# Row scatters, two pieces of expert work and a drain of Pool: one change to a fused attention and mixture-of-experts kernel

## The chip, the cores and the metric

The kernel runs on one core of a Trainium2 chip (trn2). The metric is device time in microseconds, from the first instruction to the last. Every run here was compared with the reference and was correct. A run counts as fast when it lies within 1.5% of the fastest run of the same kernel, else as slow. The ratio of two kernels is the mean time of one kernel's fast runs over that of the other's of the same rounds, so it isn't quite the ratio of the medians quoted beside it. A ratio below 1 means that the new kernel is faster; the brackets hold a 95% interval.

One thing that the text needs early, although it was only learnt from the runs: the chips that served this case came in two kinds. The kernel before takes 196 us on one kind and 235 us on the other. The words "fast chip" and "slow chip" below mean these two kinds and have nothing to do with fast and slow runs. No chip was seen as both kinds, and one (number 8) was slow in two batches 46 minutes apart; whether the cause lies in the chip or in what surrounds it, no run shows.

## The reference, cut to what matters

Block attention whose keys and values are first mixed between blocks by a Sinkhorn-normalised matrix; its output rows go through a top-1 mixture of eight experts.

```python
# attention: B, H, S, D = 4, 8, 768, 64; eight blocks of 96 positions
scores = scale * np.matmul(q_b, k_sb.transpose(0, 1, 2, 4, 3))
attn = softmax(scores)                      # the reference writes it out
x = (attn @ v_sb) -> [3072, 512]            # rows: batch and position; columns: heads
# experts: N, D, E, F = 3072, 512, 8, 1024
logits = x @ w_gate + modality_bias[modality_id]
e_idx = np.argmax(logits, axis=1)
for e in range(E):
    mask = e_idx == e
    h = np.maximum(x[mask] @ w1[e], 0.0)
    out[mask] = gate_w[mask, None] * (h @ w2[e])
```

## The kernel before

The attention is done in 32 units, eight to a group; a group is a quarter of the rows. When a group's eight units are done, its gate is computed in four parts (`gate_T` transposes a quarter of the columns, `gate_L` makes the logits), `choose` picks each row's expert, and `place(m)` computes a destination for each row and scatters the rows, with eight indirect DMAs of Pool, to a scratch array in DRAM that is sorted by expert. Slots of 256 rows of one expert are then loaded back and multiplied: `mL1` is the first expert layer, `mL2` the second, and each `mL2` ends in an indirect DMA of Pool that writes 128 rows of the result.

These pieces of expert work are spread between the attention units to fill TensorE's gaps:

```python
    def run_pieces(n):
        for _ in range(n):
            ...                               # (cut) stop if the slot's rows have not been asked for
            f(*a)
            if f is mL1 and a[1] == 3:
                st["l1"] = a[0] + 1
            if f is mL2 and a[1] == 1:
                st["done"] = a[0] + 1
            x_try()
            st["pos"] += 1

    def pace(u):
        return (0, 0) if u < 16 else (1, 0)

    for u in range(2, 32):
        p1, p2 = pace(u)
        scores(u)
        expo(u)
        run_pieces(p1)
        for f, a in A1.get(u, []):            # gate_L, place, ...
            f(*a)
        av(u - 1)                             # product op, norm xb = op * rs
        prep_q(u + 2)
        prep_s(u + 3)
        run_pieces(p2)
        for f, a in A2.get(u, []):            # gate_T: transposes gt of xb
            f(*a)
    run_pieces(1)
    av(31)
    gate_L(3, 2)
    run_pieces(2)
    gate_T(3, 3)
    run_pieces(1)
    gate_L(3, 3)
    choose(3)
    run_pieces(2)
    place(3)
    run_pieces(2)
    table_x(3)
    run_pieces(8)
    # (cut) a branch that is rarely taken, then the rest of the pieces
```

And the scatters of one group, with padding between them that is meant to have "rows leave at an even pace":

```python
        def one(t):
            if t:
                if m:
                    for _ in range(11):
                        nc.gpsimd.nop(nofuse=True)
                nc.gpsimd.nop()
            ins = nc.gpsimd.indirect_dma_start(
                out=xs_dram, out_offset=bass.IndirectOffsetOnAxis(ap=dest[:, t:t + 1], axis=0),
                in_=xt.bitcast(I32)[:, t], in_offset=None)
        for t in range(8):
            one(t)
```

The softmax here doesn't subtract the row's maximum and nothing guards it: scores larger than these inputs give would overflow.

## Time and profile before

| | us |
|---|---|
| median of three runs | 234.14 (233.84 to 235.94) |
| span of the profiled run | 191.1 |
| TensorE's last product in that run | ends at 181.6 |
| end of that product to end of program | 9.5 |

The page of the profiled run gives busy tenths in 40 equal slices of the span (some 4.8 us each), and below them the clock that the throttle granted TensorE:

```profile
span 191.1 us, 5316 instructions
PE   6594597888499989899799999987999999999900
POOL 7921296970075103576057741776044223232320
PEclk9969969999859999999999999999999999999975
```

The reader is to see that TensorE is busy for 7 tenths or more of every slice from the 12th (some 53 us) on, at nine tenths of the clock or more from the 13th, until two slices of nothing at the end. The 43 us between the span and the median were unexplained when the prediction was made. By all later runs they are two chips: the profile came from a fast one, the three timed runs from a slow one (the record gives no chip numbers for these first runs, so this is read from their times). The record of the profile already said something: its own execution was timed at 192.78 us, only 1.7 above its span.

### The profile page before, as it was taken

The page shows a single profiled execution, that of the slowest core. Times are in us where ns is not written, and L with a number is a line of the kernel's source. Part 1 is how long each engine was busy: PE and PEld are TensorE (multiplying, and loading weights), DVE is VectorE, ACT ScalarE, POOL GpSimd, SP SyncE. Part 2 cuts the span into 40 slices and gives each one's busy share as a digit, 9 for nine tenths or more (in the row PEclk, how much of TensorE's full clock was granted, in tenths as well). Part 3 has the DMA queues.
Part 4 walks back from the last instruction along what each step waited for, and adds up shares of the span by engine and source line. Part 5 has one row for each costly group of instructions (what it writes and reads, how often), then busy time and mean ns, then how long its engine had stood idle before and what let it go on. Part 6 is the DMA issues. An engine that isn't in the chain of part 4 may idle for free.

```text
span 191.1 us, 5316 instructions
## 1 busy us (share of the span) xinstructions
PE 160.8 (84%) x2127; PEld 122.1 (64%) x2127; DVE 100.6 (53%) x332; ACT 93.4 (49%) x149; POOL 83.3 (44%) x118
## 2 busy tenths in 40 slices
PE   6594597888499989899799999987999999999900
PEld 6484496766398967578568775746676676674400
DVE  4878667975557977856676535712332133232110
ACT  3135468766759968677468633631223222222300
POOL 7921296970075103576057741776044223232320
PEclk9969969999859999999999999999999999999975
DMA  3999999999999347994922376858467381212110
GB/s 49 207 212 231 184 215 210 230 193 224 209 205 259 88 75 114 184 238 134 162 66 79 86 211 123 192 150 160 131 165 167 116 82 67 98 55 105 63 55 0
DMA packets 30162, 27.69 MB, mean 145 GB/s; under 512 B 18831, under 2 KB 25775, under 8 KB 29872
## 3 DMA queue, kind: packets, MB, share of 16 engines
q0 software_dynamic: 11792, 23.10, 54.3%
q1 hardware_dynamic: 18336, 4.16, 14.2%
q8 instruction: 19, 0.31, 0.6%
q14 instruction: 15, 0.12, 0.2%
HBM read 27.35 MB, written 10.52 MB: 198 GB/s over the span
## 4 chain that ended last, share of the span: by engine, by line
PE 31%; issue 21%; DMA 18%; DVE 14%; POOL 10%; POOLq 1%; DVEq 0%
DMA kvb<-in_v_dram 9%; DMA xs_scratch<-xb,dest 9%; POOL out_dram L707 7%; PE yp L716 6%; DVE xb L444 5%; PE va L374 5%; PE hp L693 5%; PE gt L453 4%; PE op L436 4%; PE sc L417 3%; PE lg L463 2%; DVE v_sb L352 1%; DVE rs L443 1%; POOL xs_scratch L537 1%; PE tq L236 1%
## 5 line engine op out<-in xcount | busy, mean ns | idle before, releaser
L693 PE MATMUL hp<-xT,w 128*128 128x256 bf16 x384 | 46.8, 273 | 2.0 <-PEq L1001 1.9
L707 POOL DMA_INDIRECT out_dram<-kvb,idg x25 | 24.5, 981 | 47.3 <-DVE kvb L705 16.9
L693 PEld LDWEIGHTS <-w 128*128 128x128 bf16 x384 | 36.3, 98 | 10.1 <-issue 2.4
L537 POOL DMA_INDIRECT xs_scratch<-xb,dest x32 | 29.4, 919 | 29.9 <-issue 26.8
L423 ACT ACTIVATE attnT<-sc 96x768 bf16<-96x768 f32 x32 | 25.9, 810 | 7.1 <-PE sc L417 7.1
L444 DVE TENSOR_TENSOR xb<-op,rs 96x512 bf16<-96x512 f32 x32 | 22.0, 687 | 1.2
L716 PE MATMUL yp<-w,qT 128*128 128x512 bf16 x96 | 22.5, 379 | 0.0
L716 PE MATMUL yp<-w,hT 128*128 128x512 bf16 x96 | 22.5, 379 | 0.0
L703 ACT ACTIVATE kvb<-yp,idg 128x512 f32<-128x512 f32 x15 | 10.3, 687 | 20.4 <-PE yp L716 19.4
L705 DVE TENSOR_SCALAR kvb<-yp,idg 128x512 f32<-128x512 f32 x9 | 6.8, 751 | 18.7 <-PE yp L716 18.7
L687 ACT ACTIVATE hT<-hp 128x512 bf16<-128x512 f32 x18 | 10.7, 596 | 11.1 <-PE hp L693 10.8
L436 PE MATMUL op<-v_sb,attnT 96*128 96x65 bf16 x256 | 13.6, 196 | 3.0 <-DVE xb L444 2.4
L687 ACT ACTIVATE qT<-hp 128x512 bf16<-128x512 f32 x14 | 8.3, 595 | 15.6 <-PE hp L693 15.5
L716 PEld LDWEIGHTS <-qT 128*128 128x128 bf16 x96 | 9.1, 98 | 9.3
L374 PE MATMUL va<-bd,kvb 128*128 128x128 bf16 x128 | 13.6, 271 | 1.6 <-DMA kvb<-in_v_dram 1.6
L716 PEld LDWEIGHTS <-hT 128*128 128x128 bf16 x96 | 9.1, 98 | 9.1
L685 DVE TENSOR_SCALAR qT<-hp 128x512 bf16<-128x512 f32 x10 | 6.9, 691 | 13.8 <-PE hp L693 13.8
L374 PEld LDWEIGHTS <-kvb 128*128 128x128 bf16 x128 | 12.6, 194 | 1.9 <-DMA kvb<-in_v_dram 1.7
L352 ACT CAST kT<-ka 128x512 bf16<-128x512 f32 (+1 forms) x17 | 9.9, 640 | 7.0 <-PE ka L365 7.0
L436 PEld LDWEIGHTS <-attnT 96*128 96x128 bf16 x256 | 10.7, 100 | 3.9 <-DVE xb L444 2.9
L352 ACT CAST v_sb<-va 96x512 bf16<-96x512 f32 (+1 forms) x19 | 10.9, 611 | 4.6 <-PE va L374 3.9
L242 ACT COPY qT<-tq 128x768 bf16<-128x768 bf16 x14 | 11.1, 793 | 4.0 <-PE tq L236 2.8
(182 smaller groups left out, 227.6 us busy)
## 6 DMA issues: line engine op xcount, KB each, us to landing
w<-in_moe_w_dram POOLq DMA_DIRECT2D x4, 1024.0 KB
kvb<-in_k_dram POOLq DMA_DIRECT2D x4, 768.0 KB
kvb<-in_v_dram POOLq DMA_DIRECT2D x2, 1536.0 KB
q_in<-in_q_dram POOLq DMA_DIRECT2D x4, 384.0 KB
xs_scratch<-zpad SPq DMA_DIRECT2D x3, 258.0 KB, 3.6
v_sb<-in_q_dram POOLq DMA_DIRECT2D x4, 192.0 KB
v_sb<-in_q_dram POOLq DMA_DIRECT2D x2, 384.0 KB
xs_scratch<-xb,dest POOLq DMA_INDIRECT x32
```

The lines of the kernel that those rows point to most:

```text
L242: eng(qT, tq.pop(u).rearrange("p t (i r) -> p i t r", r=16))
L352: (nc.scalar.copy if pick(act, dve) else nc.vector.tensor_copy)(dst, src)
L374: nc.tensor.matmul(acc[:, z], v_cols[:, d0 + z], bd[g], start=True, stop=True)
L423: mark[0] = nc.scalar.activation(attnT[u % 2][:, 0:8 * BLK].rearrange("p (r f) -> p r f", r=2), sc_tiles.pop(u)[0:BLK, :, 0:4 * BLK], ACT. ...
L436: nc.tensor.matmul(ov[:, par, j], attnT[u % 2][:, c0:c0 + 128], v_sb[g][0:BLK, par * 64 + h * 8 + i, 0:D + 1], start=True, stop=True)
L444: nc.vector.tensor_tensor(xt[:, :, h * D:(h + 1) * D].rearrange("p (r j) d -> p r j d", r=2), ov[0:BLK, :, :, 0:D], rs.broadcast_to([BLK, ...
L537: ins = nc.gpsimd.indirect_dma_start(out=xs_dram, out_offset=bass.IndirectOffsetOnAxis(ap=dest[:, t:t + 1], axis=0), in_=xt.bitcast(I32)[: ...
L687: mark[0] = nc.scalar.activation(dst, src, ACT.Relu)
L693: nc.tensor.matmul(hp[:, f], w_at(s, c * F + (2 * j + f) * 128, 128), xT_b[s % NX][:, c], start=(c == 0), stop=(c == 3))
L703: nc.scalar.activation(dst, src, ACT.Copy, scale=gate)
L707: ins = nc.gpsimd.indirect_dma_start(out=out, out_offset=bass.IndirectOffsetOnAxis(ap=idg[:, t, 0:1], axis=0), in_=y, in_offset=None, boun ...
L716: nc.tensor.matmul(yp, hT_b[s % 2][:, fc, t * 128:(t + 1) * 128], w_at(s, 4 * F + fc * Dm, Dm), start=(fc == 0), stop=(fc == 7))
```

## The change

Its intent: close two waits at the gate in units 16 and 24; give the last group's gate an earlier start; replace the padding between scatters by something that takes time; and let Pool do the work of a drain (a queue instruction whose record lasts, in these traces, at least until its engine is through with the work in front of it) early, where it is idle, and not at the end of the program. The diff, whole but for context:

```diff
+    pause = nc.gpsimd.alloc_register("pause")
...
-                    for _ in range(11):
-                        nc.gpsimd.nop(nofuse=True)
+                    for _ in range(2):
+                        nc.gpsimd.reg_load(pause, etab[0:1, 0:1])
...
+            if f is mL2 and a == (9, 1):
+                nc.gpsimd.drain()
...
     def pace(u):
-        return (0, 0) if u < 16 else (1, 0)
+        return (0, 0) if u < 16 else (1, 0) if u % 8 else (0, 1)
...
     run_pieces(1)
+    gate_L(3, 2)
     av(31)
-    gate_L(3, 2)
-    run_pieces(2)
+    run_pieces(1)
     gate_T(3, 3)
     run_pieces(1)
     gate_L(3, 3)
     choose(3)
     run_pieces(2)
     place(3)
-    run_pieces(2)
+    run_pieces(3)
     table_x(3)
```

So there are four parts: the drain, the units, the tail and the loads.

## The prediction

> **What bounds the kernel now.** I read the windows by stage first, then the gaps of TensorE in the timeline, then the chain of waits, and last the queue instructions after the last output row. The chain names "issue" and Pool for its last 50 us, which misleads: there Pool only follows TensorE. The windows say so (columns: stretch, its length, busy us of PE, weight loads, DVE, ACT, POOL, granted clock, DMA share, GB/s).
>
> ```profile
> 99.00:119.00 20.00, 19.77 (x250) 14.46 (x248) 10.60 (x39) 12.11 (x19) 10.91 (x13) 1.00 0.50 131
> 119.00:132.00 13.00, 11.10 (x86) 8.08 (x85) 4.83 (x27) 4.99 (x9) 9.64 (x12) 1.00 0.66 171
> 132.00:182.00 50.00, 49.13 (x328) 31.46 (x325) 14.04 (x20) 14.59 (x24) 14.56 (x15) 1.00 0.44 104
> 182.00:191.00 9.00, 0.00 (x0) 0.00 (x0) 0.48 (x1) 0.11 (x1) 0.98 (x1) 0.62 0.08 29
> ```
>
> TensorE is all but full from 85 to 181.6 us, at full clock. So in that stage only TensorE's gaps are worth anything, and after it 9 us follow in which nothing computes. The gaps over 0.8 us from 64 us on are three:
>
> ```profile
> 70.79 0.52 PE L453 MATMUL gt<-ident,xb 96*128 96x96 bf16 x8 [0.82 <-DVE xb L444]
> 91.84 0.51 PE L453 MATMUL gt<-ident,xb 96*128 96x96 bf16 x8 [1.16 <-DVE xb L444]
> 130.02 3.65 PE L693 MATMUL hp<-xT,w 128*128 128x256 bf16 x32 [1.90 <-PEq L1001]
> ```
>
> The first two are units 16 and 24: the gate's transpose waits for the norm of the unit before it. On VectorE ahead of the second one stand these three:
>
> ```profile
> 90.13 0.69 DVE L685 TENSOR_SCALAR qT<-hp 128x512 bf16<-128x512 f32 x1 [0.32 <-PE hp L693]
> 90.86 0.20 DVE L443 RECIPROCAL rs<-op 96x8 f32<-96x8 f32 x1
> 91.09 0.69 DVE L444 TENSOR_TENSOR xb<-op,rs 96x512 bf16<-96x512 f32 x1
> ```
>
> TensorE finished its last product before the gate at 90.68 and sat until the norm was written at 91.78. The third gap is the branch around the rare extra slots, which the change leaves alone.
>
> The end of the kernel, in the chain of waits and in the queue instructions of the closing line (x count: min/median/max ns, first and last start):
>
> ```profile
> 182.91 0.98 POOL L707 DMA_INDIRECT out_dram<-kvb,idg  x1 [1.06 <-DVE kvb L705]
> L1032 POOLq DRAIN  x3: 46/109/7582, 182.7 to 190.8; - x3
> L1032 SPq EVENT_SEMAPHORE  x13: 17/28/21660, 163.5 to 191.1; - x13
> L1032 SPq DRAIN  x3: 7/7/13, 185.9 to 190.5; - x3
> ```
>
> SyncE waited 21.66 us from 163.5, to 185.2, for the output rows; the trace has the last landing at 185.18, and no DMA packet starts later. SyncE is through at 185.94. Pool's drain, which began at 182.68, lasts 7.58 us, to 190.26. Pool's last counted instruction ended at 183.89. So for 190.26 - 185.94 = 4.3 us the kernel waits for nothing but this drain; the closing barrier then takes 0.8 us to 191.1.
>
> **What the Trainium skill says.** "VectorE: DVE Perf Modes", section "The DRAIN you can't avoid", puts the drains of preamble and postamble at some 12 ns on all engines. SyncE's (7 to 13 ns) agree; Pool's 7582 ns doesn't, and the measurement decides: this drain is doing or awaiting something. "Perfetto Trace Analysis", section "Sequencer-only Instruction (DRAIN, etc)", says that the profile shows execution alone, not the wait for semaphores; so 7.58 us is no semaphore wait. The same page, section "DMA Instruction — SWDGE (GPSIMD)", ends the record of such a DMA when the descriptors are written, before the DSP has completed the instruction: work of the DSPs may lie hidden after each row scatter, and the long drain fits that, though nothing here proves it. "DMA: Bandwidth & Descriptors", section "Latency and other measured facts", gives a register load a floor of about 600 ns; this trace has less on Pool, below.
>
> **The change part by part.**
>
> Drain in slot 9. It removes no data movement. It stands behind the 20th of 25 output rows, which started on Pool at 167.73 and ended at 168.71. Between rows Pool idles about 2.4 of every 3.5 us. If the early drain costs as much as the last one after its row (190.26 - 183.89 = 6.4 us), Pool is free again near 175.1. The rows that started at 171.13 and 174.68 then go at about 175.1 and 176.4, the next at 177.7 instead of 177.26, and those of 180.87 and 182.91 are on time. TensorE isn't held: eight y buffers are four slots of slack, and at most three rows pile up. So the early drain costs about 0. What it saves depends on what the last drain does. If its length grows with the indirect DMAs since the previous drain, five rows are left of 25 (or of 57 with the row scatters): 6.4 x 5/25 = 1.3 us, or 0.6 us. It would end by 185.2, before SyncE at 185.94, and the span would fall by the whole 4.3 us. If it is a fixed time after the last DMA, it saves 0.
>
> Units 16 and 24. The piece (8 matmuls, 0.87 us of TensorE) moves from ahead of the gate to between the norm's product and the gate's transpose. In unit 16 TensorE has 0.34 (logits) + 0.27 (product) + 0.34 (transposes of q) + 0.87 (piece) before the transpose; the norm will be ready about 1.9 us after the unit's scores, against 1.8 of work: the gap of 0.82 shrinks to about 0.05, a gain of 0.8. In unit 24 there are no q transposes: product done at about 89.65, accumulate, reciprocal and norm end near 90.8, the piece ends at 90.5: 0.3 of 1.16 stays, a gain of 0.8. The piece's relu now follows the norm on VectorE, which also takes 0.69 us out of the norm's way. Sum 1.6 us, if no transfer becomes the bound: the second expert's first weights landed at 80.7 for a use at 85.4; the rows for slot 2 landed at 94.5 for 99.8; those for slot 4 at 116.7 for 119.3, and these move forward with the gate. All hold.
>
> The tail. The logits move ahead of the last unit's product, and one piece moves behind the placing: the last placing comes 0.9 us earlier. TensorE has no gap between 103 and 128 us, so nothing is won there: 0.
>
> Register loads. Eleven no-operations per gap go, two loads come. Pool's row scatters run at the same pace in the first group, which has no such padding, and in the third:
>
> ```profile
> 56.00 0.92 POOL L537 DMA_INDIRECT xs_scratch<-xb,dest  x1 [0.30 <-issue]
> 57.23 0.92 POOL L537 DMA_INDIRECT xs_scratch<-xb,dest  x1 [0.30 <-issue]
> 102.43 0.91 POOL L537 DMA_INDIRECT xs_scratch<-xb,dest  x1 [0.30 <-issue]
> 103.64 0.91 POOL L537 DMA_INDIRECT xs_scratch<-xb,dest  x1 [0.30 <-issue]
> L644 POOLq TENSOR_LOAD <-etab x3: 292/306/508, 34.1 to 61.8; - x3
> ```
>
> The spacing is 1.22 and 1.21: the padding lies hidden behind the engine's 0.91 + 0.30. In the third group the sequencer was done with all eight scatters in 4.0 us (97.66 to 101.66), 0.5 each; less perhaps 0.3 for the padding, plus 2 x 0.31 and some issue time, I estimate 0.9 each, still under 1.21. Cost 0. Were the loads not hidden, 7 x 0.6 = 4 us later rows would use up the 2.5 us of slack of slot 4 and cost 1 to 2 us.
>
> Sum on the span: 4.3 + 1.6 = 5.9 of 191.1, to 185.2. The timed median, 234.14, is 43 us above the profiled span, and the trace doesn't show why. If the 43 are constant, the result is 228.2; if the timed runs are slower by the same factor throughout (234.14/191.1 = 1.225), it is 234.14 x 185.2/191.1 = 226.9.
>
> **The rivals.**
>
> The fixed drain. The last drain may be a fixed routine, or a wait of some 5 us after the last landing, however many DMAs went before; the early drain is then paid twice and hides nothing. For it: rows are 3.5 us apart late in the kernel, time enough for Pool to clear up, and the landings lag their issue by a steady 2.6 us, no sign of a backlog. Against it: the program's first drain took 184 ns and the two after the long one 109 and 46 ns, so it isn't a cost of every drain; and someone chose this very slot, the last in which 6.4 us still fit. It leaves 1.6: 231.8 to 232.5.
>
> The early drain waits for landings, or takes longer than its cost at the end. The last rows bunch up and the landing moves past 185.2. With 8 us in place of 6.4 they would follow at 1.3 us each from 176.7 and still reach the last one in time; I give it little weight: 229 to 230.
>
> The drain is there only under the profiler. Then the timed runs gain 1.6 or so, although the traces differ by 5.9: 232.
>
> The register loads hold the engine. If each were to wait until Pool is idle, the spacing would be near 1.9 us, and slot 4's rows late: 1 to 2 us back.
>
> **Range and chances.** I hold the drain's gain at about six in ten whole, three in ten absent, one between, and the gaps' 1.6 at three in four. Whole: 226.9 to 228.2, a little more with a gap unfilled; absent: about 232. The threshold of 2% is 229.46, between these two groups. I take 228.4, between the groups but near the first; the range 225.8 to 232.8 holds both. Faster by over 2%: 0.57; within: 0.39; slower: 0.04, for loads that cost far more than reckoned.
>
> **What would show it.** Right: in the closing line's queue instructions Pool's long drain is under 2.5 us, and SyncE's wait for the rows ends last; a second long drain of about 6 us stands near 168 us less the shift, with the next two or three rows 1.3 us apart. The waits of 0.82 and 1.16 at the gate's transpose are under 0.1 and near 0.3, and TensorE's last product ends near 180 instead of 181.6. The spacing of the scatters stays at 1.2. Wrong: a closing drain still over 6 us (the fixed rival), output rows after 171 us that delay TensorE or the last landing, spacing of 1.8 us in the scatters of the later groups with a wait for slot 4's rows, or a gap that reopens at a later transpose. If the span falls by 5.9 and the time doesn't, the drain belonged to the profiler.

## The result, and the profile after

| | before | after |
|---|---|---|
| median of four runs, us | 235.04 (233.84 to 236.33) | 226.63 (224.01 to 231.41) |
| ratio of fast runs | | 0.9604 [0.9492, 0.9716] |

Faster, by 4.0%. On the 234.14 us of before the ratio makes 224.9, just below the predicted range of 225.8 to 232.8 and 3.5 us below the predicted 228.4. One of the four runs of after, 231.41, was a slow run and is not in the ratio. All outputs are right.

The profiled run of after has a span of 225.2 us and took 226.84. It is from a slow chip, the profile of before from a fast one, so the two pages can't be subtracted from one another:

```profile
span 225.2 us, 5358 instructions
PE   6574978895489998289992299981559999999990
POOL 7802879405610306611067302376020322313053
PEclk9889699878555899959998579999599999999999
```

The columns are as before. TensorE has holes in the 17th, the 22nd and 23rd, and the 28th to 30th slices that the profile of before doesn't have. They come back below. What can be compared despite the chips are stretches that the chip's kind leaves alone: the end, and the two units.

The end. These are the queue instructions of the closing line (x count: min/median/max ns, first and last start):

```profile
L1035 SPq EVENT_SEMAPHORE  x13: 17/28/21650, 202.0 to 225.1; - x13
L1035 POOLq DRAIN  x3: 46/109/2749, 221.1 to 224.9; - x3
L1035 SPq DRAIN  x3: 7/7/13, 224.3 to 224.6; - x3
```

And the new drain in slot 9:

```profile
L904 POOLq DRAIN  x1: 7174/7174/7174, 205.9 to 205.9; - x1
```

The closing drain fell from 7582 to 2749 ns, and the 7.2 us that a long one takes now stand at 205.9. From TensorE's last product to the end of the program it was 191.1 - 181.6 = 9.5 us and is 225.2 - 220.0 = 5.2. The predicted 4.3 us are there, though the closing drain is a little longer than the 2.5 us that the prediction named as its sign. Pool's rows around the early drain (start, us, in brackets the idle time before and what ended it):

```profile
206.13 0.98 POOL L708 DMA_INDIRECT out_dram<-kvb,idg  x1 [2.56 <-DVE kvb L706]
214.32 0.98 POOL L708 DMA_INDIRECT out_dram<-kvb,idg  x1 [7.21 <-ACT xTg L688]
215.61 0.98 POOL L708 DMA_INDIRECT out_dram<-kvb,idg  x1 [0.30 <-DVE kvb L706]
216.89 0.98 POOL L708 DMA_INDIRECT out_dram<-kvb,idg  x1 [0.30 <-issue]
219.28 0.98 POOL L708 DMA_INDIRECT out_dram<-kvb,idg  x1 [1.41 <-ACT kvb L704]
221.31 0.98 POOL L708 DMA_INDIRECT out_dram<-kvb,idg  x1 [1.05 <-DVE kvb L706]
```

Pool is held until 213.07; three rows then follow 1.3 us apart, as predicted, and the last two are on time: 219.28 and 221.31 each wait for the engine that makes their data.

The units. TensorE in unit 16 and in unit 24 (start, us, what; in the profile of before, the `gt` lines had their waits in brackets at the end):

```profile
77.23 0.41 PE L436 MATMUL op<-v_sb,attnT 96*128 96x65 bf16 x8
77.47 0.50 PE L236 MATMUL tq<-ident,q_il 128*128 128x128 bf16 x6
77.81 1.04 PE L694 MATMUL hp<-xT,w 128*128 128x256 bf16 x8
78.87 0.52 PE L453 MATMUL gt<-ident,xb 96*128 96x96 bf16 x8
...
106.99 0.42 PE L436 MATMUL op<-v_sb,attnT 96*128 96x65 bf16 x8
107.25 1.04 PE L694 MATMUL hp<-xT,w 128*128 128x256 bf16 x8
108.43 0.51 PE L453 MATMUL gt<-ident,xb 96*128 96x96 bf16 x8
```

The piece `hp` now fills the time in which the norm `xb` is made, and the waits of 0.82 and 1.16 us ahead of `gt` are gone. The two units' lengths, from one unit's scores to the next one's, bear it out: on slow chips 3.52 us each in n0_before, d_only, r_only and t_again (runs of the old order, told below), and 2.55 (2.75 in this run) and 2.98 in u_only, du_only, ut_again and the whole change. Gain: 0.97 + 0.54 = 1.5 us. There are exceptions: in `ut_only` unit 16 took 3.92 us, because slot 0's rows had landed late, and with spaced scatters one of the two can be longer (4.00 and 5.31 us in all_spaced1 and all_spaced2).

The loads. The trace shows none: at their line it has only the waits below, of 17 ns each (seven gaps in each of three groups, two each, are 42). The register is never read; that the build dropped the loads for this reason is likely, but not shown.

```profile
L536 POOLq EVENT_SEMAPHORE  x42: 17/17/17, 85.4 to 148.8; - x42
```

The scatters are 1.21 us apart before and after. The eleven no-operations of before leave nothing in its trace either. So this part of the change is empty, and the padding never spaced anything.

That makes 5.8 us where the fast-run ratio says 235.04 x (1 - 0.9604) = 9.3. The experiments look for the rest.

### The profile page after: what moved, and what is told of

It is laid out like the page before. It is cut to its first block, busy times and chain, and to the rows that moved or that the text cites.

```text
span 225.2 us, 5358 instructions
## 1 busy us (share of the span) xinstructions
PE 175.3 (78%) x2127; PEld 128.0 (57%) x2127; DVE 100.9 (45%) x332; ACT 93.4 (41%) x149; POOL 83.4 (37%) x118
## 4 chain that ended last, share of the span: by engine, by line
issue 27%; PE 27%; DMA 19%; POOL 10%; DVE 7%; another core or an unknown queue 6%; POOLq 2%; ACT 1%; DVEq 0%; ACTq 0%
DMA xs_scratch<-xb,dest 11%; DMA kvb<-in_v_dram 8%; POOL out_dram L708 5%; PE yp L717 5%; PE va L374 5%; PE hp L694 4%; PE sc L417 4%; PE gt L453 3%; DVE xb L444 3%; PE op L436 3%; POOL xs_scratch L538 3%; PE lg L463 2%; PE tq L236 1%; DVE v_sb L352 1%
## 5 line engine op out<-in xcount | busy, mean ns | idle before, releaser
L694 PE MATMUL hp<-xT,w 128*128 128x256 bf16 x384 | 48.7, 278 | 5.6 <-issue 3.3
L538 POOL DMA_INDIRECT xs_scratch<-xb,dest x32 | 29.5, 922 | 31.4 <-issue 29.4
L717 PE MATMUL yp<-w,hT 128*128 128x512 bf16 x96 | 26.6, 425 | 7.7 <-ACT hT L688 7.7
L688 ACT ACTIVATE hT<-hp 128x512 bf16<-128x512 f32 x17 | 10.0, 595 | 27.1 <-PE hp L694 9.6
L704 ACT ACTIVATE kvb<-yp,idg 128x512 f32<-128x512 f32 x14 | 9.6, 688 | 22.8 <-PE yp L717 18.3
L417 PE MATMUL sc<-qT,kT 64*128 64x96 bf16 (+1 forms) x256 | 13.4, 220 | 6.1 <-issue 4.9
L436 PE MATMUL op<-v_sb,attnT 96*128 96x65 bf16 x256 | 14.7, 203 | 3.9 <-DVE xb L444 2.4
L374 PE MATMUL va<-bd,kvb 128*128 128x128 bf16 x128 | 14.8, 288 | 3.6 <-issue 2.0
L688 ACT ACTIVATE qT<-hp 128x512 bf16<-128x512 f32 x16 | 9.5, 595 | 18.2 <-PE hp L694 18.1
L374 PEld LDWEIGHTS <-kvb 128*128 128x128 bf16 x128 | 13.3, 188 | 4.0 <-issue 2.2
L453 PE MATMUL gt<-ident,xb 96*128 96x96 bf16 x128 | 10.2, 230 | 5.6 <-DVE xb L444 4.4
L436 PEld LDWEIGHTS <-attnT 96*128 96x128 bf16 x256 | 11.5, 104 | 4.7 <-DVE xb L444 2.9
L352 ACT CAST v_sb<-va 96x512 bf16<-96x512 f32 (+1 forms) x19 | 10.8, 611 | 6.6 <-PE va L374 6.0
```

Of the source, the lines that this page charges most:

```text
L352: (nc.scalar.copy if pick(act, dve) else nc.vector.tensor_copy)(dst, src)
L374: nc.tensor.matmul(acc[:, z], v_cols[:, d0 + z], bd[g], start=True, stop=True)
L417: nc.tensor.matmul(sc[0:m, par, j * BLK:(j + 1) * BLK], kT[g][rows, x0:x0 + m], qT[rows, i], start=True, stop=True)
L436: nc.tensor.matmul(ov[:, par, j], attnT[u % 2][:, c0:c0 + 128], v_sb[g][0:BLK, par * 64 + h * 8 + i, 0:D + 1], start=True, stop=True)
L453: nc.tensor.transpose(tp[:, t], xb[m % 2][:, t, c * 128:(c + 1) * 128], ident[:BLK, :BLK])
L538: ins = nc.gpsimd.indirect_dma_start(out=xs_dram, out_offset=bass.IndirectOffsetOnAxis(ap=dest[:, t:t + 1], axis=0), in_=xt.bitcast(I32)[: ...
```

## The experiments

The theory: drain and units are worth 4.3 and 1.5 us wherever the kernel runs, and the rest comes of the tail on slow chips. The first rival: one of the four parts is worth much more than its stretch shows. The second: the rest is chance of the runs.

The runs came in five batches; each batch's kernels ran on one chip with the kernel before beside them. The fourth batch (spaced_again to all_fourth) ran on the same chip as the first, which was slow both times. Beside the ratio, "product to branch" is the stretch from TensorE's last attention product (unit 31) to the branch ahead of the rare extra slots; the tail's work lies within it.

| run | chip | median, us | before, us | ratio of fast runs | product to branch, us |
|---|---|---|---|---|---|
| n0_before | slow | 237.21 | 237.17 | 1.0043 [0.9939, 1.0146] | 29.5 |
| d_only | slow | 232.73 | 237.17 | 0.9753 [0.9631, 0.9876] | 29.6 |
| u_only | slow | 232.61 | 237.17 | 0.9859 [0.9769, 0.9948] | 29.5 |
| r_only | slow | 236.28 | 237.17 | 0.9982 [0.9868, 1.0096] | 29.5 |
| t_only | fast | 197.48 | 196.3 | 1.0088 [1.0024, 1.0151] | 17.1 |
| ut_only | fast | 193.24 | 196.3 | 0.9847 [0.9769, 0.9926] | 17.1 |
| all_again | fast | 189.27 | 196.3 | 0.9603 [0.9515, 0.9692] | 17.2 |
| spaced | fast | 200.59 | 196.3 | 1.0267 [1.0176, 1.0357] | 22.2 |
| du_only | slow | 229.91 | 235.05 | 0.9802 [0.9704, 0.9901] | 29.3 |
| all_third | slow | 227.91 | 235.05 | 0.9672 [0.9567, 0.9777] | 27.8 |
| t_again | slow | 233.80 | 235.05 | 1.0061 [1.0002, 1.0120] | 27.4 |
| drains_many | slow | 234.36 | 235.05 | 1.0076 [0.9984, 1.0167] | 29.4 |
| spaced_again | slow | 209.33 | 234.87 | 0.8933 [0.8857, 0.9010] | 22.0 |
| all_spaced2 | slow | 205.33 | 234.87 | 0.8795 [0.8721, 0.8869] | 19.3 |
| ut_again | slow | 231.77 | 234.87 | 0.9841 [0.9785, 0.9897] | 27.7 |
| all_fourth | slow | 226.98 | 234.87 | 0.9727 [0.9643, 0.9811] | 27.5 |
| all_spaced2_all | fast | 189.34 | 196.54 | 0.9664 [0.9606, 0.9721] | 17.3 |
| all_spaced1 | fast | 189.90 | 196.54 | 0.9689 [0.9638, 0.9740] | 17.1 |

The same stretch is 27.1 in the first profile of after (slow chip) and 17.4 in that of before (fast chip).

### The kernel before against itself

No edit.

> The kernel before against itself: ratio 1.00, interval within 0.99 to 1.01 if the method is sound. It also shows the kernel before in the state in which the timed runs fall: if they all have a span near 232 us and a clock near 0.88, with gaps of TensorE that no instruction accounts for, the first profile at 191.1 us was the exception, and the 43 us between them are stalls that both kernels have.

1.0043, with 1.0 in the interval, which is about 1% wide on either side. A difference of 2 us is thus at the edge of what one comparison can tell. The kernel before ranged from 233.46 to 239.47 us in this batch alone. In part this goes with the granted clock: of these eleven runs the two at a mean clock of 0.861 had spans of 231.8 and 233.2 us, the one at 0.833 had 237.8. This is why stretches of the traces are used beside the times.

### The parts one by one

The drain alone:

```diff
+            if f is mL2 and a in ((9, 1), ):
+                nc.gpsimd.drain()
```

> The drain in slot 9 alone. If the last drain grows with the indirect DMAs since the one before: closing drain under 3 us, time lower by 4.3 us, ratio 0.98. If the last drain is of fixed length: closing drain over 6 us, ratio 1.00. If the drain has a further effect in the middle of the kernel: a ratio under 0.975.

0.9753, some 5.9 us (only two of its six runs count as fast). The closing drain took 2.75 us. TensorE's last product to the end of the program is 5.2 us (230.8 - 225.65) against 9.5 (235.8 - 226.3) in n0_before: the drain is worth 4.3 us on the slow chip too, and in the runs' times as in the trace. So it isn't a thing of the profiler.

The units alone:

```diff
-        return (0, 0) if u < 16 else (1, 0)
+        return (0, 0) if u < 16 else (0, 1) if u in (16, 24) else (1, 0)
```

> The pieces of units 16 and 24 alone. My theory: the two gaps at the gate's transpose close, time lower by 1.6 us, ratio 0.993. The rival, that TensorE's gaps are worth more in the slower state because the throttle stretches them: 3 us or more, ratio under 0.988.

0.9859, 3.3 us with an interval of 1.2 to 5.5. That is the rival's figure, but the trace doesn't bear the rival out: the two units' lengths fell by 0.97 and 0.54, together 1.5, about what the theory said, and the interval holds this too.

The register loads alone:

```diff
-                    for _ in range(11):
-                        nc.gpsimd.nop(nofuse=True)
+                    for _ in range(2):
+                        nc.gpsimd.reg_load(pause, etab[0:1, 0:1])
```

> The register loads alone (the trace of the changed kernel shows no load there, only two semaphore updates of 17 ns per gap). My theory: nothing, ratio 1.00 within 0.3%. The rival, that the padding spreads the row scatters or shifts what the engines fetch beside them, and that this is the part that I missed: 3 us or more, ratio under 0.988.

0.9982: nothing, as is fit for a part that isn't in the built program.

The tail alone, on a fast chip, with the order of calls as in the change's last hunk:

```diff
     run_pieces(1)
-    av(31)
     gate_L(3, 2)
-    run_pieces(2)
+    av(31)
+    run_pieces(1)
 ...
     place(3)
-    run_pieces(2)
+    run_pieces(3)
```

> The tail's reordering alone: the last logits ahead of the last unit's product, one piece behind the last placing. My prediction put it at 0, ratio 1.00, since TensorE had no gap there. The rival, from the trace of the changed kernel: between the last unit's product and the branch it is 2.4 us shorter than in the kernel before (27.1 against 29.5), because in the timed runs the engines nearly stand still while the last group of row scatters goes out: 2.4 us, ratio 0.990.

1.0088: no gain, and 0.9% the wrong way. The stretch is 17.1 us against 17.4. On the fast chip the tail is worth nothing, as predicted. Some of the loss stands right behind the branch: from there to TensorE's last product it took 56.8 us, where the profile of before has 55.2, with TensorE idle for 1.28 us at 136.70 ahead of a relu of ScalarE. ut_only has the same tail and took 55.6.

Units and tail together, on that chip:

> Units 16 and 24 and the tail together, with the padding as before and no drain. If the parts add up: the units' 0.986 times the tail's ratio. With a tail worth nothing 0.986, with one of 2.4 us 0.976.

0.9847, 3.0 us [1.5 to 4.5]; the stretches say 0.5 us in unit 24, none in unit 16 (see above), 0.3 in the tail. The time gained more than these say.

The whole change again, on that chip:

> The whole change once more, on this chip. If the parts add up and the tail is worth nothing: 0.975 x 0.986 = 0.961; with a tail of 2.4 us 0.951. With the prediction's own sizes for drain (4.3 us) and units (1.6 us) it would be 0.975.

0.9603: 7.8 us of 196.3 [6.1 to 9.5]. The gain in microseconds is about the same on the two kinds of chip. And the 43 us are not added by the timing: each profiled run's time is some 1.7 us above its span (188.93 and 187.3 here, 226.84 and 225.2 in the first profile of after), so on a slow chip they lie within the span. The end of this run, 187.3 - 182.1 = 5.2 us, and the units' 2.55 and 2.99 us are as on the slow chip. TensorE's last product, however, didn't come near 180 as the prediction had it: from branch to last product this run took 57.2 us for 55.2, with a granted clock of 0.62 and then 0.81 between 128.9 and 134.9, where the profile of before has 1.00 behind its branch.

### Why the tail differs between chips

With the scatters of the last group as landmark, the stretch falls in two. From product to first scatter it takes 9.33 or 9.34 us in the traces without the tail's new order (10.9 and 10.8 in spaced and spaced_again, whose scatters are spaced), and 7.75 to 7.77 in every one with it, on both kinds of chip. So the gate is earlier by 1.58 us everywhere, and the question is what becomes of it. The windows of before, on the fast chip, from product to first scatter and on to the branch (stretch, length, busy us of PE, weight loads, DVE, ACT and Pool, granted clock, DMA share, GB/s):

```profile
109.00:118.30 9.30, 9.30 (x95) 6.45 (x94) 4.71 (x18) 3.90 (x7) 2.65 (x4) 1.00 0.65 162
118.30:126.40 8.10, 8.10 (x57) 5.28 (x55) 3.39 (x25) 3.86 (x7) 6.27 (x7) 1.00 0.81 190
```

TensorE is busy for the whole 17.4 us. An earlier scatter frees nothing. Now r_only, which is the kernel before in all but 17 ns waits, in a fast run on a slow chip; the second window holds the eight scatters, the third goes from there to the branch:

```profile
140.10:149.40 9.30, 9.25 (x94) 6.50 (x94) 4.70 (x18) 3.88 (x7) 2.17 (x3) 1.00 0.29 86
149.40:158.00 8.60, 5.08 (x41) 3.65 (x38) 3.40 (x25) 1.41 (x3) 6.43 (x8) 1.00 0.46 134
158.00:169.60 11.60, 5.78 (x14) 1.89 (x16) 0.00 (x0) 2.37 (x4) 3.83 (x4) 0.56 0.37 109
```

Up to the first scatter it is the same. Then TensorE executes 41 matmuls and in the next 11.6 us only 14, at a clock of 0.56; VectorE does nothing at all. The core is near to standing still. This is what it looks like instruction by instruction in that run (the first four lines are of ACT and PE, the last of DVE):

```profile
159.45 0.60 ACT L688 ACTIVATE hT<-hp 128x512 bf16<-128x512 f32 x1 [7.39 <-remote]
160.50 0.63 PE L717 MATMUL yp<-w,hT 128*128 128x512 bf16 x1 [6.03 <-ACT hT L688]
163.80 1.09 ACT L688 ACTIVATE hT<-hp 128x512 bf16<-128x512 f32 x2 [3.75 <-remote]
164.45 5.29 PE L717 MATMUL yp<-w,hT 128*128 128x512 bf16 x12 [3.31 <-ACT hT L688]
169.78 0.75 DVE L706 TENSOR_SCALAR kvb<-yp,idg 128x512 f32<-128x512 f32 x1 [14.54 <-PE yp L717]
```

ScalarE's relu of 0.6 us waits 7.39 us for something that the trace calls remote, TensorE waits for the relu, and VectorE waits for TensorE. In the table work before the hole, VectorE needs 0.69 us ahead of an operation that depends on the one just before it, where the earlier ones of that chain start 0.19 us apart:

```profile
154.26 0.15 DVE L609 TENSOR_REDUCE tb_t<-rem 1x1 f32<-1x8 f32 x1
155.10 0.14 DVE L610 CAST nrem<-tb_t 1x1 int32<-1x1 f32 x1 [0.69 <-DVE tb_t L609]
```

The same hole stands behind the scatters of the earlier groups: units 20 and 21 together take 13.7 to 15.4 us in the slow chip's traces with scatters 1.21 us apart, and 6.07 on the fast one; unit 29 takes 8.6 to 11.5 and 2.25. The fast chip has no such hole.

In the last group everything up to the branch then hangs on the scatters: from first scatter to branch it takes 20.0 to 20.2 us on the slow chip with the old order and 19.3 to 20.0 with the new. The tail's 1.58 us are passed on. This was the reading of the first traces; it could be an accident of one profile, so the tail was run again on a slow chip.

> The order of the last pieces alone. Theory A: on a slow chip (before at about 236 us) 2.4 us less, ratio 0.990, product of unit 31 to branch 27.1 us instead of 29.5; on a fast chip (before at about 196 us) no gain, ratio 1.00. Rival B (the 27.1 of the whole change on the slow chip was chance, or came of the earlier units): the stretch stays at 29.5 on a slow chip too. The earlier run of this kernel on a fast chip was 0.9% slower; if that was real it comes back at 1.009, if it was chance it is 1.00.

The windows of t_again (fast run), as above:

```profile
136.70:144.50 7.80, 7.80 (x85) 5.59 (x84) 4.19 (x17) 3.76 (x7) 2.21 (x4) 1.00 0.22 72
144.50:153.00 8.50, 6.30 (x47) 4.27 (x46) 3.95 (x26) 1.88 (x3) 6.37 (x8) 0.99 0.59 157
153.00:164.10 11.10, 5.72 (x17) 1.94 (x18) 0.13 (x1) 1.77 (x3) 3.83 (x4) 0.55 0.37 108
```

27.4 us from product to branch against 29.5: theory A's stretch. The time, however, doesn't show it: 1.0061, not 0.990, and nearer to the 1.009 of the fast chip. The medians lean the other way (233.80 and 235.05), which says how little one comparison can tell of 2 us. So the trace carries the theory and the time of this kernel doesn't. In the same batch:

> The drain of slot 9 and the pieces of units 16 and 24, without the tail and without the register loads. Theory A (the tail earns its 2.4 us only on a chip that stands still during the row scatters): on a chip whose kernel before takes about 196 us the gain is that of the whole change, ratio 0.96 to 0.97, product of unit 31 to branch about 17 us; on a chip whose kernel before takes about 236 us it is 5.8 us, ratio 0.975, and that stretch stays at 29.5 us. Rival B (drain and units are worth no more than 5.8 us anywhere, and the rest of the whole change's gain on the fast chip comes from the tail): ratio 0.970 on the fast chip, and at least 0.007 above that of all_third.

> The whole change again, beside the others of this call: ratio 0.960, between 0.950 and 0.970. On a slow chip product of unit 31 to branch 27.1 us, on a fast one 17.2.

du_only has everything but the tail (and the empty loads): 0.9802, and 29.3 us of stretch. all_third has the tail: 0.9672, and 27.8. The difference of 0.013 is 3 us, in the direction of theory A and of its size or more, but the intervals overlap. Over all traces of the slow chip the stretch is 29.3 to 29.6 us in the six without the new order (n0_before, d_only, u_only, r_only, du_only, drains_many) and 27.1 to 27.8 in the five with it (after, all_third, t_again, ut_again, all_fourth), means 29.5 and 27.5. The two sets don't touch: 2.0 us.

### Many drains

Meant as the whole change with five more drains. By a slip it was built on the kernel before, so it has six drains, the old order of the units and the old tail; the expectation's sentence on the time doesn't apply to it. What it says of the drains' lengths does.

```diff
+            if f is mL2 and a in ((1, 1), (3, 1), (5, 1), (7, 1), (9, 1), (11, 1), ):
+                nc.gpsimd.drain()
```

> The whole change with five more drains of Pool, behind slots 1, 3, 5, 7 and 11. Theory A (a drain costs about 1.1 us after its row's end and 0.09 us for each indirect DMA since the drain before): the first, behind slot 1 with some 36 DMAs before it, ends about 4.3 us after its row's end, each later one 1.3 to 1.6 us, the closing one about 1.3; the one of slot 9 falls from 5.96 to 1.5. The time is that of the whole change within 1%. Rival B (a fixed time after a long gap or a landing): each drain ends 5 to 6 us after its row, and the closing one too, with the time 2 to 4 us up.

```profile
L903 POOLq DRAIN  x6: 3048/3218/9822, 125.1 to 225.4; - x6
```

The last four of these six had four indirect DMAs each between them and the drain before, and lasted 3.0 to 3.3 us; the closing one had one, and lasted 2.57. Together with the other runs: 57 indirect DMAs since the program's start make 7.58 us (before, n0_before, u_only, t_again, ut_again, spaced_again), 52 make 7.17, 5 make 2.75. The drain in slot 9 fell from 7.17 us to 3.15 when others had gone before it. So a drain's length goes with the indirect DMAs since the last drain, by (7.58 - 2.75) / 52 = 0.09 us each, and rival B's fixed 5 to 6 us is out. The first two, in slots 1 and 3, lasted 9.82 and 9.77 us, because they began (125.1 and 155.5) while other DMAs were still queued ahead of them. So a drain is better counted from the end of the row in front of it (130.91 and 162.96 for these two). Counted so, it takes 6.4 us after 57 indirect DMAs, 6.0 after 52, 4.0 after 28, 2.3 after 12, 1.8 to 2.1 after 4 (slots 5 to 11), 1.6 after 5 and 1.4 after one: near theory A's 1.1 + 0.09 for each, with up to 0.6 more. Six drains bring nothing: 1.0076. The one behind slot 11 holds up the last row, which starts 3.0 us after TensorE's last product (229.33 - 226.36) where it is 1.3 in the other kernels. The rest of the loss was not traced.

### Spacing the scatters

If scatters 1.21 us apart are what halts a slow chip, real padding should cure it. The padding here is a memset of Pool into a tile that nobody reads.

```diff
-                if m:
-                    for _ in range(11):
-                        nc.gpsimd.nop(nofuse=True)
+                if m in (1, 2, 3):
+                    for _ in range(5):
+                        nc.gpsimd.memset(spc, 0.0)     # spc: [128, 128] FP32
```

> The kernel before with five short memsets on Pool (about 1.3 us) between the row scatters of the later three groups, so that a group takes about 18 us in place of 9.7. In the timed runs TensorE, VectorE and ScalarE nearly stand still from the middle of each group to about 3 us after its end. If the density of the scatters causes it, the standstill goes and the time falls by 5 to 20 us, ratio under 0.97. If it lasts as long as a group is going out, each of three groups costs up to 8.5 us more, ratio 1.04 to 1.11. If the two have nothing to do with each other, the later rows alone cost some 1 to 6 us.

On the fast chip, 2.35 us of spacing cost 2.7%: there is no hole to cure there, and the last rows come later. A later batch landed on a slow chip:

> The kernel before with five memsets of Pool between the row scatters of groups 1 to 3, which widens their spacing from 1.21 to about 2.35 us (only groups after the first; the earlier run of it was on a fast chip and 2.7% slower, as the last placing's rows came 8 us later). Theory A (on a slow chip it is the close spacing of the scatters that makes all engines stand still until 4.8 us after a group's last one): on a chip whose kernel before takes about 235 us, units 20 with 21 and unit 29 go back from 14.7 and 12.5 us towards 6.1 and 2.3, and the time falls by 10 us or more, ratio under 0.96. Rival B (each scatter holds the engines up for its share, at whatever spacing, or the cause isn't the scatters): the standstill stays or grows longer with the group, ratio 1.02 or more. On a fast chip: 1.027 again, and nothing is told apart.

0.8933, 25 us faster. Units 20 and 21 take 6.07 us, unit 29 takes 2.77, both near the fast chip's figures. Theory A held, rival B is out. (All spacing here was made with memsets, so whether the time between scatters or the memset itself does it was not told apart.) With the whole change, and two memsets in place of the two loads that never ran:

```diff
                     for _ in range(2):
-                        nc.gpsimd.reg_load(pause, etab[0:1, 0:1])
+                        nc.gpsimd.memset(spc, 0.0)
```

> The whole change with two memsets of Pool (0.22 and 0.20 us) between the scatters of groups 1 to 3 in place of the register loads that aren't in the built program: spacing about 1.65 us. It is what the padding was meant to be. Theory A: on a slow chip it beats the whole change by 5 us or more. Rival B: it is 1 to 3 us slower than the whole change there. On a fast chip about 2 us slower than the whole change (7 gaps of 0.4 us in the last group).

0.8795: 205.33 us where the whole change beside it takes 226.98. Pool in the last group (start, us, what, idle before):

```profile
132.03 0.93 POOL L538 DMA_INDIRECT xs_scratch<-xb,dest  x1 [3.43 <-issue]
132.95 0.49 POOL L536 MEMSET spc<- 128x128 f32 x2
133.60 0.91 POOL L538 DMA_INDIRECT xs_scratch<-xb,dest  x1 [0.16 <-issue]
```

The scatters are 1.57 us apart, and the windows from product to first scatter to branch (a run marked slow, so no better than its kind) are:

```profile
124.30:132.00 7.70, 7.70 (x80) 5.53 (x81) 4.11 (x17) 3.63 (x7) 2.17 (x3) 1.00 0.68 172
132.00:143.60 11.60, 9.73 (x63) 5.74 (x62) 4.17 (x27) 3.76 (x6) 10.03 (x22) 1.00 0.58 153
```

63 matmuls after the first scatter, at full clock, where r_only had 41 and then 14. The closing drain of spaced_again is 7584 ns with 105 memsets more on Pool, so it counts indirect DMAs and not Pool's instructions, nor the time that has passed.

Its companions in the batch:

> Units 16 and 24 with the tail, without the drain. If the parts add up as the traces' stretches say (units 1.5, tail 2.1 on a slow chip and 0 on a fast one): ratio 0.985 on a slow chip, 0.992 on a fast one (the earlier fast run gave 0.9847, 3 us). Rival (the parts help one another, so that units and tail together give more than their sum): 0.98 or less.

0.9841, 27.7 us of stretch, as the sum of the parts says (0.985).

> The whole change once more, as measure for the others of this call: mean of all its runs 7.5 us under that of the kernel before, on either kind of chip; product of unit 31 to branch 27 to 28 us on a slow chip, 17.2 on a fast one; ut_again lies 4.3 us above it, as the drain alone is worth that.

0.9727, and 27.5 us. The expectation speaks of the means of all runs, fast and slow: 227.06 against 234.80, 7.7 us under, with ut_again at 231.71, 4.7 above. That is near the drain's 4.3.

Last, the spacing in the first group too, and a smaller one:

```diff
-                if m:
+                if True:
                     for _ in range(2):
                         nc.gpsimd.memset(spc, 0.0)
```

> As all_spaced2 (whole change, two memsets between scatters), but in the first group too, where scatters are still 1.22 us apart and units 10 and 11 still took 7.8 and 6.3 us on a slow chip against 4.1 and 3.3 on a fast one. Theory A (close spacing makes the engines stand still): on a slow chip units 10 and 11 fall to about 4 and 3.5, less up to 3 us as the first group ends 3 us later, so 3 to 6 us under all_spaced2's 205. Rival B (the first group's slowness is the throttle after 62 us, not the scatters): units 10 and 11 stay, and the time is that of all_spaced2 or up to 3 us above. On a fast chip 2 to 5 us above the whole change.

> As all_spaced2 with one memset in place of two: spacing some 1.4 us in groups 1 to 3. If the standstill comes of a backlog that each scatter adds to when the next one follows in less than some 1.3 to 1.5 us, most of the gain is there already on a slow chip (205 or a little less, units 20 with 21 near 6.1); if it shrinks in proportion to the spacing, about half of the gain (215). On a fast chip within 1% of the whole change.

Both landed on a fast chip, where the questions that they were to settle have no answer. They show one useful thing: 0.9664 and 0.9689, and medians of 189.34 and 189.90 us against 189.27 of the whole change in its own batch on such a chip. The 2 to 5 us that the first expectation gave the fast chip didn't come: spacing by 1.57 or 1.3 us costs it no more than these runs can tell. all_spaced2 is thus the version to keep: 12% under the kernel before on a slow chip; on a fast one it was not run itself, but the kernel that spaces one more group was 3.4% under it.

## Why the prediction was right or wrong

| step of the prediction | predicted, us | fast chip | slow chip |
|---|---|---|---|
| drain in slot 9 | 4.3 | 4.3 | 4.3 |
| units 16 and 24 | 1.6 | 1.5 | 1.5 |
| tail | 0 | 0.3 | 2.0 |
| register loads | 0 | 0 | 0 |
| sum of stretches | 5.9 | 6.1 | 7.8 |
| gain by ratios of fast runs | | 7.8 | 9.3, 7.7, 6.4 |

The last row works out as before's median times (1 - ratio): all_again for the fast chip; the first result, all_third and all_fourth for the slow one, mean 7.8. Much of the spread between the three comes from which runs the 1.5% limit keeps: over all runs, fast and slow, the means differ by 7.9, 7.6 and 7.7 us (7.0 on the fast chip).

The drain: right, in size and in kind. The rival that the length is fixed, the one that the drain waits for landings, and the one that it exists only under the profiler all fell: the length goes with the indirect DMAs since the last drain, the rows followed as worked out, and d_only gained in its times. One step of the reasoning was not sound, and did no harm: the prediction took it that 7.58 us can be no semaphore wait, as a record shows execution alone; but the same fence has a semaphore instruction of SyncE with a recorded 21.66 us, which is a wait. And of the 7.58 us only 6.4 come after the last row; the first 1.2 pass while Pool still works on it.

The units: right, 1.5 for 1.6, with the split 0.97 and 0.54 in place of 0.8 and 0.8.

The loads: right in the number, wrong in the reason. They are not hidden behind the engine's pace; in the trace they don't run at all.

The tail: this step failed. "TensorE has no gap between 103 and 128 us, so nothing is won there: 0." It is true of the chip on which the profile was taken and false of the chip on which the time was taken. On the latter TensorE stands nearly still behind the scatters, the way to the branch runs through the scatters and not through TensorE, and the 1.58 us by which the gate comes earlier, with some 0.4 more behind it, are won in that stretch: 27.5 us for 29.5. That they are won in the time as well is not shown: t_again by itself gained nothing, and the intervals of du_only and all_third overlap.

The two readings of the 43 us failed with it. A constant and a factor were considered; a third, another chip with another bound, was not, although the profiled execution's own time, 192.78 us, already spoke against a constant of the timing. The term 4.3 + 1.6 could be carried over because it doesn't depend on the chip. The term 0 could not.

And the centre was drawn back: 228.4 hedges between a gain that is there (226.9 to 228.2) and one that isn't (232). The first branch with the tail's 2.0 added and the units' 0.1 taken off, 234.14 - 7.8 = 226.3, is inside the range. The first comparison's 9.3 us lies above the mean of three such comparisons, 7.8, by what their intervals allow. So of the 3.5 us by which 224.9 lies under 228.4, the tail's stretch accounts for 2.0, and 9.3 - 7.8 = 1.5 is what the first comparison has over the mean of the three; the hedge and the units' 0.1 nearly cancel. Most of this 1.5 hangs on one run: with the slow run of 231.41 counted in, the two means differ by 7.9. So the tail's zero is the step that failed, but alone it would not have carried the result out of the range.

What stays open: why close scatters halt a slow chip and not a fast one (a "remote" wait and slow dependent operations are the signs; no run shows the mechanism); what makes a chip slow or fast; whether the first group has the hole too (units 10 and 11 take 14 to 15 us on the slow chip and 7 on the fast one, and no spaced first group was run on a slow chip); why the tail alone doesn't show in the time of t_again and costs 0.9% in t_only; and the 1.7 us by which the fast chip's gain exceeds its stretches, at the edge of its interval.

## What to carry to other kernels

When the profiled span and the timed median differ by more than a few per cent, find out whether they come from the same chip before any gap in the profile is called worthless: a bound read from one chip may not hold on another, and only savings that don't depend on the bound carry over. Look in the built program or the trace for what padding has become; here eleven no-operations and two loads per gap were nothing, and 0.5 us of real work per gap was worth 22 us on one kind of chip. Where Pool issues many indirect DMAs, a drain in an idle stretch late in the program takes most of the closing one off the end.

## What the Trainium skill lacked or had wrong

- "VectorE: DVE Perf Modes", section "The DRAIN you can't avoid", gives boilerplate drains as some 12 ns on all engines. Here SyncE's took 7 to 13 ns, but Pool's closing one 7582 ns after 57 indirect DMAs, 7.17 us after 52 and 2749 ns after 5: about 0.09 us for each since the last drain. The page doesn't have this dependence; these drains are recorded at a line of the program, so they may not be the boilerplate that it means. The closing drains of TensorE, ScalarE and VectorE weren't short either: in the profile of before they took up to 1817, 504 and 524 ns, from 179.8, 181.6 and 182.2, and so end with their engine's last instruction (181.6, 182.1, 182.6).
- "DMA: Bandwidth & Descriptors", section "Latency and other measured facts", gives a register load a floor of about 600 ns. The three on Pool here took 292, 306 and 508 ns.
- On no page I found: row scatters by indirect DMA 1.21 us apart can bring all engines nearly to a halt. On the slower chips, units 20 and 21 took 13.7 to 15.4 us together beside such scatters, and 6.07 with scatters 1.57 us apart; the kernel's time went from 226.98 to 205.33.
- On no page I found: chips of one type differ this much. The same kernel took 196 us on two chips and 235 to 237 on two others, and how much a part of a change took off its stretch depended on which: the tail 0.3 us and 2.0.
